# Scores of two heads from the two row halves of the array, in an attention-and-MoE kernel on one core

## The chip, the cores and the metric

The kernel runs on one core of one Trainium2 chip. The core has a TensorE (PE in the profile) with its weight loads shown apart (PEld), a VectorE (DVE), a ScalarE (ACT), a GpSimd (POOL), and a SyncE (SP), whose queue issues all DMAs here. The metric is device time in microseconds, from the median of several runs.

## What is computed

Causal attention with a decay (8 batches, 8 heads, 576 tokens, head dimension 64) is followed by a feed-forward layer (512 to 2048 to 512) over all 4608 tokens, called the MoE in the code.

```python
def _attn_ref(q, k, v, f):
    scale = 1.0 / np.sqrt(D)
    scores = scale * np.matmul(q, k.transpose(0, 1, 3, 2))
    cum = np.cumsum(np.log(np.clip(f, 0.0001, 1.0)), axis=-1)
    decay = cum[:, :, :, None] - cum[:, :, None, :]
    scores = np.where(causal, -1000000000.0, scores + decay)
    ...
    attn = attn / (np.sum(attn, axis=-1, keepdims=True) + 1e-09)
    return np.matmul(attn, v)

def _moe_ref(x, w_in, w_out):
    h = x @ w_in
    g = np.where(pos, h, np.where(neg, 0.0, (h + beta) ** 2 / (4.0 * beta)))
    return g @ w_out
```

## The kernel before

**Jobs.** Two heads of a batch make a pair; a pair is a job, except in batch 0, whose pairs are cut into rows 0 to 255 and 256 to 575 (`CUTS`). That makes 36 jobs. The first 12 (`NQK`) compute their scores in float32, the other 24 in float16 from split operands: each number is a high float16 plus a low float16 that holds the rest.

**A job's stages.** `load` (L311) brings q and k of both heads into `x32`. `measure` (L385) finds the scale of q and k. `prepare` (L408) splits them into `qs` and turns `qs` with a transposing DMA into `qkT` (L430), so that the head dimension lies on partitions; the float32 jobs do this in `early_prepare` (L362) with TensorE transposes and copies by ScalarE (L381, L383). `scores(w, r)` (L466) makes row tile r of 128 query rows against all keys up to it: 128, 256, 384 or 512 columns for r = 0 to 3, each head into its own tile `s` in PSUM; the last row tile, r = 4, has 64 rows a head and 576 columns, and both heads share one tile `big`, head 0 on partitions 0 to 63 and head 1 on 64 to 127. GpSimd prepares the decay and the mask for the same tile (L496, L500). `weights` (L565) adds the two, takes the exponential and the sum, splits the result and turns it with another transposing DMA into `pT` (L609). `values` (L616) multiplies by v, the two heads into two column halves of the array.

**Score products before.** In float16, q of a head lies as high on rows 0 to 63 and low on rows 64 to 127; k lies doubled, the high part on both row halves and the low part on both (`kk`, doubled by the copy at L427). Two products of 128 rows then give all four terms (L492):

```python
for c in range(2):
    nc.tensor.matmul(
        sp[p0:p1, c0:c1], lhsT=w.q[:, h, ...],
        rhs=w.k[:, c, h, c0:c1], start=(c == 0), stop=(c == 1),
    )
```

In float32, k of the two heads lies stacked on the two row halves, and q of each head stands in its half of a buffer whose other half is zero (zeroed once, at L360), so one product of 128 rows gives one head (L486).

**MoE.** Work comes in units (`moe_front`, L650, with its products at L665, and `moe_back`, L686, products at L693). Units are handed out between the steps of the attention as tokens become ready; what is left runs after the last pair. The weights are split during the first jobs (`weight_split`, L188).

**What sets the order.** The code is written in the order of the loop at L765, with the next pair's preparation ahead of a pair's scores. A scheduler then orders each engine's instructions by priority and by when it expects buffers to be free. Every engine works in its order, and SP's queue issues DMAs in its order. The tile `s` has two buffers in PSUM, so the next row tile's scores wait until DVE has read the ones before (L579).

## Time and profile before

| | |
|---|---|
| median of 3 runs | 1213.34 us (1212.29 to 1214.77) |
| span of the profiled execution, first to last instruction | 1209.7 us |
| mean granted clock of TensorE | 0.941 |
| PE by slices of a fortieth of the span (tenths busy) | `4677678996598989999999999999799989999998` |
| score products, float16 (L492) | 576, from 291 to 1038 us |
| score products, float32 (L486) | 192 records, from 14 to 278 us |

The profiled execution has no time of its own beside its span; the runs' times lie a few microseconds above it. In the profile a line such as "L492 PE MATMUL s<-qkT 128\*128 128x512 f16" names the source line, the engine, what is written and read, the part of the array used (rows by columns), and the output's size. A row half is 64 rows of the array; a column half is 64 of its columns. A float32 product shows as two records.

### The profile page before, as it was taken

Reading aid. Unit: us, or ns where it says so; the run is one execution under the profiler, and the core shown is the slowest. Engines: PE = TensorE matmul, PEld = TensorE weight load, DVE = VectorE, ACT = ScalarE, POOL = GpSimd, SP = SyncE. Lnnn points to the kernel's source line nnn. Section 1 sums busy time; section 2 is a strip of 40 time slices with the busy share of each in tenths; the row PEclk is TensorE's granted clock in tenths of the full one; section 3 lists DMA queues with packets and bytes.
Section 4 is the critical chain, followed back from the end, with each engine's and each line's share of the span. In section 5 each row is a group of like instructions: output and inputs, shape, how many; then the busy total and the mean of one; then the engine's idle time right before and its main releaser. Section 6 shows DMA issues by size and latency. Waiting matters only on the chain. (4 is left out here: it accounts for less than half of the span.)

```text
span 1209.7 us, 24371 instructions
## 1 busy us (share of the span) xinstructions
PE 1074.8 (89%) x8577; PEld 707.0 (58%) x8577; DVE 865.9 (72%) x2447; ACT 766.1 (63%) x1570; POOL 445.6 (37%) x699
## 2 busy tenths in 40 slices
PE   4677678996598989999999999999799989999998
PEld 3454344663366656665666666666566666667665
DVE  6879979775887788877766867877878788532222
ACT  4675666774576677767666767776667587643443
POOL 5648634533444334423433234433543264100000
PEclk9878788998599998999899999999899989999999
DMA  8857544569787859685666656894969686400000
GB/s 239 255 170 178 133 121 96 122 131 193 158 159 130 172 119 179 130 181 124 133 131 138 137 106 142 160 190 106 179 117 189 127 161 113 96 18 2 18 18 18
DMA packets 439258, 160.04 MB, mean 132 GB/s; under 512 B 414944, under 2 KB 415968, under 8 KB 439136
## 3 DMA queue, kind: packets, MB, share of 16 engines
q1 hardware_dynamic: 439136, 158.49, 61.2%
q8 instruction: 67, 1.10, 0.4%
q14 instruction: 55, 0.45, 0.1%
HBM read 75.64 MB, written 9.58 MB: 70 GB/s over the span
## 5 line engine op out<-in xcount | busy, mean ns | idle before, releaser
L665 PE MATMUL ph<-x,place 128*128 128x256 f16 (+3 forms) x4608 | 454.2, 251 | 15.9 <-DVE u L676 8.7
L693 PE MATMUL po<-place,g 128*128 128x512 f16 x1728 | 423.6, 383 | 12.0 <-DVE g L679 5.9
L665 PEld LDWEIGHTS <-place 128*128 128x128 f16 x4608 | 371.7, 100 | 99.8 <-issue 25.1
L693 PEld LDWEIGHTS <-g 128*128 128x128 f16 x1728 | 162.9, 98 | 179.1 <-DVE g L679 10.5
L496 POOL TENSOR_SCALAR sdr<-ck,nsig,cqs 128x128 f32<-128x128 f32 (+1 forms) x192 | 161.0, 842 | 200.4 <-DVE pr L603 184.3
L583 ACT ACTIVATE sdr<-sdr,nm 128x384 f32<-128x384 f32 (+1 forms) x248 | 138.2, 558 | 105.7 <-DVE nm L579 99.0
L676 DVE SCALAR_TENSOR_TENSOR u<-ph,z,u 128x512 f32<-128x512 f32 x136 | 101.3, 745 | 106.2 <-ACT u L675 105.6
L674 ACT ACTIVATE u<-ph,z 128x512 f32<-128x512 f32 x136 | 104.5, 768 | 92.6 <-PE ph L665 92.5
L678 ACT ACTIVATE g<-u,z 128x512 f16<-128x512 f32 x136 | 97.6, 717 | 91.7 <-DVE u L676 91.5
L597 ACT ACTIVATE pr<-sdr,rc 128x384 f16<-128x384 f32 (+1 forms) x236 | 119.2, 555 | 44.3 <-issue 19.2
L496 POOL TENSOR_SCALAR sd<-ck,nsig,cqs 64x576 f32<-64x576 f32 x48 | 50.7, 1057 | 259.2 <-DMA ck<-cum_d 77.1
L603 DVE SCALAR_TENSOR_TENSOR pr<-sdr,rc,pr 128x384 f16<-128x384 f32 (+2 forms) x232 | 124.2, 568 | 14.7 <-ACT pr L597 14.0
L679 DVE SCALAR_TENSOR_TENSOR g<-u,z,g 128x512 f16<-128x512 f32 x136 | 105.9, 779 | 37.7 <-ACT g L678 37.3
L579 DVE CUSTOM_DVE_ANT_0 sdr<-s,sdr,nalpha 128x128 f32<-128x128 f32 (+1 forms) x192 | 102.4, 543 | 20.5 <-PE s L492 10.2
L492 PE MATMUL s<-qkT 128*128 128x128 f16 (+3 forms) x384 | 87.2, 320 | 24.0 <-DVE nm L579 13.6
L500 POOL TENSOR_SCALAR_AFFINE_SELECT sdr<-sdr 128x128 f32<-128x128 f32 x248 | 92.8, 386 | 9.6
L675 ACT ACTIVATE u<-u 128x512 f32<-128x512 f32 x144 | 89.9, 625 | 2.9
L492 PEld LDWEIGHTS <-qkT 128*128 128x128 f16 (+1 forms) x576 | 47.3, 104 | 66.5 <-issue 43.7
L623 PE MATMUL big<-pT,vs 128*64 128x320 f16 (+3 forms) x1098 | 74.7, 286 | 5.5 <-DVE nm L579 4.6
L392 DVE TENSOR_REDUCE m2q<-qk 128x1 f32<-128x640 f32 x48 | 39.1, 817 | 50.4 <-DMA qk<-in_q_dram 26.1
L623 PEld LDWEIGHTS <-vs 128*64 128x64 f16 x1098 | 53.4, 113 | 32.6 <-issue 13.4
L496 POOL TENSOR_SCALAR sdr<-ck,cq 128x384 f32<-128x384 f32 (+3 forms) x56 | 40.0, 714 | 67.5 <-DVE pr L603 23.3
(168 smaller groups left out, 1180.6 us busy)
## 6 DMA issues: line engine op xcount, KB each, us to landing
ck<-cum_d SPq DMA_DIRECT2D x64, 288.0 KB, 3.8
out_dram<-ot SPq DMA_DIRECT2D x36, 256.0 KB, 2.4
qk<-in_k_dram SPq DMA_DIRECT2D x64, 128.0 KB, 2.9
ck<-in_v_dram SPq DMA_DIRECT2D x28, 288.0 KB, 3.1
v<-in_v_dram SPq DMA_DIRECT2D x62, 128.0 KB, 2.6
qk<-in_q_dram SPq DMA_DIRECT2D x56, 128.0 KB, 2.7
place<-in_moe_w_in_dram SPq DMA_DIRECT2D x12, 512.0 KB, 4.9
place<-in_moe_w_out_dram SPq DMA_DIRECT2D x10, 512.0 KB, 6.3
```

What stands on the lines that cost most here:

```text
L492: nc.tensor.matmul(sp[p0:p1, c0:c1], lhsT=w.q[:, h, q0 - w.s0:q0 - w.s0 + p1 - p0], rhs=w.k[:, c, h, c0:c1], start=(c == 0), stop=(c == 1),)
L496: nc.gpsimd.tensor_scalar(out=sd[p0:p1, 0:wid], in0=w.ck[h][p0:p1, 0:wid], scalar1=w.nsig if w.p < NQK else w.nsig[p0:p1], scalar2=w.cqs[p ...
L579: nc.vector.tensor_tensor_reduce(out=a, in0=sp[:, 0:wid], in1=a, scale=w.nalpha, scalar=BIG, op0=ALU.add, op1=ALU.min, accum_out=nm[:, i:i ...
L583: nc.scalar.activation(a, a, AF.Exp, bias=nm[:, i:i + 1], scale=-1.0, accum_out=sm[:, i:i + 1])
L597: nc.scalar.activation(pr[:, :, 0, i, :], a, AF.Copy, scale=rc[:, i:i + 1])
L603: nc.vector.scalar_tensor_tensor(out=pr[:, :, 1, i, :], in0=a, scalar=rc[:, i:i + 1], in1=pr[:, :, 0, i, :], op0=ALU.mult, op1=ALU.subtract,)
L623: nc.tensor.matmul(av[64 * h:64 * h + 64, at + s0:at + s1], lhsT=w.vs[:, vl, h, t, :], rhs=w.pT[:, t, pl, h, s0:s1], start=(t == 0 and pi ...
L665: nc.tensor.matmul(ph[:, fi, a0:a1], lhsT=wi[fb][:, wl, t, fi * P:(fi + 1) * P], rhs=xs[b][:, t, xl, s0:s0 + a1 - a0], start=(fi == 0 and ...
L674: nc.scalar.activation(u, h, AF.Relu, scale=z.u[:, i:i + 1], bias=z.h[:, i:i + 1])
L676: nc.vector.scalar_tensor_tensor(out=u, in0=h, scalar=z.t[:, i:i + 1], in1=u, op0=ALU.max, op1=ALU.min)
L679: nc.vector.scalar_tensor_tensor(out=g[:, 1], in0=u, scalar=z.r[:, i:i + 1], in1=g[:, 0], op0=ALU.mult, op1=ALU.subtract)
L693: nc.tensor.matmul(po[ch][i], lhsT=g[:, gl, fi * TC + i * P:fi * TC + (i + 1) * P], rhs=wo[fb][:, wl, fi, :], start=(first and fi == 0 and ...
```

## The change

In float16, `qs` now has four blocks of 640 columns: q high, q low, k high, k low, each with the two heads side by side, so that after the transposing DMA head 0 lies on rows 0 to 63 and head 1 on rows 64 to 127. A head's scores are three products of 64 rows (high by high, low by high, high by low; the term low by low is no longer computed), head 0 in the upper row half of the array and head 1 in the lower. In float32 q and k lie stacked alike and one product of 64 rows makes a head. The doubled k with its copy, the zeroed halves with their memsets, and the copies of half height go. The transposing DMA of a pair has 20 blocks of 128 by 128 instead of 30. In `scores` the products of both heads are written in turn, ahead of the GpSimd work of both. `load` puts the float16 jobs' q and k into the layout of the float32 ones (token tile, head, dimension).

```diff
@@ load
-            if ji < NQK:
-                dst = x.rearrange("p (t h d) -> p h t d", t=nt, h=2)
-            else:
-                dst = x.rearrange("p (h t d) -> p h t d", t=nt, h=2)
-                if ji < max(NQK, ncut) + 2 and w.r1 == NT5:
-                    nc.gpsimd.memset(dst[64:P, :, nt - 1, :], 0.0)
+            dst = x.rearrange("p (t h d) -> p h t d", t=nt, h=2)
+            if NQK <= ji < max(NQK, ncut) + 2 and w.r1 == NT5:
+                nc.gpsimd.memset(dst[64:P, :, nt - 1, :], 0.0)
...
-    early_qk = [two.tile([P, 3, 2, SP], F16, name="qkT") for i in range(2)]
+    early_qk = [two.tile([P, 4, SP], F16, name="qkT") for i in range(2)]
...
-    for t in early_qk:
-        for h in range(2):
-            nc.gpsimd.memset(t[64 - 64 * h:128 - 64 * h, h, :], 0.0)
@@ early_prepare
-        w.q, w.k = t_, t_[:, 2]
+        w.terms = ((t_[:, 0], t_[:, 1]),)
...
-            if j == 0:
-                for h in range(2):
-                    rows = slice(64 * h, 64 * h + 64)
-                    nc.scalar.activation(t_[rows, h, 0:n], pt[rows, 0:n], AF.Copy)
-            else:
-                nc.scalar.activation(t_[:, 2, 0:n], pt[:, 0:n], AF.Copy)
+            nc.scalar.activation(t_[:, j, 0:n], pt[:, 0:n], AF.Copy)
@@ prepare
...
-        dup = kk.rearrange("p c b e -> p (c b) e")
-        nc.vector.tensor_copy(dup[:, :, D:P], dup[:, :, 0:D])
...
+        qs = one.tile([P, 4, NT5 * P], F16, name="qs")
+        for j in range(2):
+            nc.scalar.activation(qs[:, 2 * j], w.x32[j], AF.Copy, scale=sc[:, j:j + 1])
+        for j in range(2):
+            nc.vector.scalar_tensor_tensor(
+                out=qs[:, 2 * j + 1], in0=w.x32[j], scalar=sc[:, j:j + 1], in1=qs[:, 2 * j],
+                op0=ALU.mult, op1=ALU.subtract,
+            )
+        qkT = two.tile([P, 4, SP], F16, name="qkT")
+        nc.sync.dma_start_transpose(
+            qkT.rearrange("p c (b e) -> p (c b) e", e=P), qs.rearrange("p c e -> p (c e)")
+        )
+        qh, ql, kh, kl = (qkT[:, c] for c in range(4))
+        w.terms = ((qh, kh), (ql, kh), (qh, kl))
@@ scores
-            for c0 in range(0, wid, 512):
-                c1 = min(wid, c0 + 512)
-                if w.p < NQK:
...
-                for c in range(2):
-                    nc.tensor.matmul(
-                        sp[p0:p1, c0:c1], lhsT=w.q[:, h, q0 - w.s0:q0 - w.s0 + p1 - p0],
-                        rhs=w.k[:, c, h, c0:c1], start=(c == 0), stop=(c == 1),
-                    )
+        for c0 in range(0, wid, 512):
+            c1 = min(wid, c0 + 512)
+            for i, (a, b) in enumerate(w.terms):
+                for h, (p0, p1) in enumerate(at):
+                    rows = slice(64 * h, 64 * h + 64)
                     nc.tensor.matmul(
+                        sds[h % len(sds)][1][p0:p1, c0:c1], lhsT=a[rows, q0 - w.s0:q0 - w.s0 + p1 - p0],
+                        rhs=b[rows, c0:c1], start=(i == 0), stop=(i == len(w.terms) - 1),
                     )
+        for h, (p0, p1) in enumerate(at):
+            sd = sds[h % len(sds)][0]
```

What the scheduler makes of it on PE, at row tile r = 2 (384 columns) of the ninth float16 pair. `qkT` holds the pair's q and k, the two tiles `s` are head 0's and head 1's, `g` and `po` belong to the MoE. Before:

```order
L492 LDWEIGHTS qkT_6491
L492 MATMUL s_6984<-qkT_6491 128x384
L492 LDWEIGHTS qkT_6491
L492 MATMUL s_6984<-qkT_6491 128x384
L693 LDWEIGHTS g_7242
L693 MATMUL po0_6677<-place13_103,g_7242 128x512
L492 LDWEIGHTS qkT_6491
L492 MATMUL s_6991<-qkT_6491 128x384
L492 LDWEIGHTS qkT_6491
L492 MATMUL s_6991<-qkT_6491 128x384
```

And in the change, on the same engine at the same place:

```order
L470 MATMUL s_7058<-qkT_6550 128x384
L470 LDWEIGHTS qkT_6550
L470 MATMUL s_7058<-qkT_6550 128x384
L470 LDWEIGHTS qkT_6550
L470 MATMUL s_7058<-qkT_6550 128x384
L673 LDWEIGHTS g_7324
L673 MATMUL po0_6744<-place13_103,g_7324 128x512
L470 LDWEIGHTS qkT_6550
L470 MATMUL s_7059<-qkT_6550 128x384
L470 LDWEIGHTS qkT_6550
L470 MATMUL s_7059<-qkT_6550 128x384
L470 LDWEIGHTS qkT_6550
```

Although the code writes the heads in turn, head 0's three products stand together, then a product of the MoE (L673 is L693 of before), then head 1's three.

Row tile r = 0 (128 columns) of the same pair, on PE in the change, where `ph` is the MoE's (L645 is L665 of before):

```order
L645 MATMUL ph_7295<-x_3196,place12_102 128x256
L470 LDWEIGHTS qkT_6550
L470 MATMUL s_7010<-qkT_6550 128x128
L470 LDWEIGHTS qkT_6550
L470 MATMUL s_7011<-qkT_6550 128x128
L470 LDWEIGHTS qkT_6550
L470 MATMUL s_7010<-qkT_6550 128x128
L470 LDWEIGHTS qkT_6550
L470 MATMUL s_7011<-qkT_6550 128x128
```

Here the heads alternate, as written, with nothing between them; before, two products of each head stood there one after the other.

On DVE, where the same pair is split into `qs`, before:

```order
L420 SCALAR_TENSOR_TENSOR qs_6485<-qk32_0_114,sc_6397,qs_6485 128x10x64
L404 RECIPROCAL nalpha_6405<-nsig_6403 128x1
L423 SCALAR_TENSOR_TENSOR qs_6485<-qk32_0_114,sc_6397,qs_6485 128x10x64
L427 COPY qs_6485<-qs_6485 128x20x64
L676 SCALAR_TENSOR_TENSOR u_6458<-ph_6409,z_5528,u_6458 128x512
```

And in the change:

```order
L405 SCALAR_TENSOR_TENSOR qs_6545<-qk32_0_114,sc_6457,qs_6545 128x640
L559 ISA sdr_2_119,nm_6617<-s_6568,sdr_2_119,nalpha_5948 128x256
L559 ISA nm_6617 128x1
L405 SCALAR_TENSOR_TENSOR qs_6545<-qk32_0_114,sc_6457,qs_6545 128x640
L571 TENSOR_SCALAR rc_6592<-sm2_6587 128x2
```

The two subtractions stay, each over 640 columns in one piece; the doubling copy is gone, and a reading of scores (L559, L579 of before) now stands between the two.

More of the change, by code (lines that the diff above doesn't have):

```diff
@@ L354 @@
     prs = [one.tile([P, PRN[r]], F16, name=f"pr{r}").bitcast(F32) for r in range(NT5)]
-    early_qk = [two.tile([P, 3, 2, SP], F16, name="qkT") for i in range(2)]
-    early_qk = [t.rearrange("p c h s -> p (c h s)").bitcast(F32)[:, 0:3 * S].rearrange("p (c s) -> p c s", c=3) for t in early_qk]
+    early_qk = [two.tile([P, 4, SP], F16, name="qkT") for i in range(2)]
+    early_qk = [t.rearrange("p c s -> p (c s)").bitcast(F32)[:, 0:2 * S].rearrange("p (c s) -> p c s", c=2) for t in early_qk]
     cq8 = const.tile([P, NT5, 2 * H], F32, name="cq8")
-    for t in early_qk:
-        for h in range(2):
-            nc.gpsimd.memset(t[64 - 64 * h:128 - 64 * h, h, :], 0.0)
     def early_prepare(w):
@@ L411, in prepare @@
         sc = w.sc
-        nq, nk = w.r1 - w.r0, w.r1
-        qs = one.tile([P, 3, 2, NT5, P], F16, name="qs").rearrange("p c h t e -> p (c h t e)")
-        nqe = 2 * nq * P
-        qq = qs[:, 0:nqe].rearrange("p (b e) -> p b e", e=P)
-        kk = qs[:, nqe:nqe + 4 * nk * P].rearrange("p (c b e) -> p c b e", c=2, e=P)
-        xq, xk = (x.rearrange("p (b d) -> p b d", d=D) for x in w.x32)
-        nc.scalar.activation(qq[:, :, 0:D], xq, AF.Copy, scale=sc[:, 0:1])
-        nc.scalar.activation(kk[:, 0, :, 0:D], xk, AF.Copy, scale=sc[:, 1:2])
-        nc.vector.scalar_tensor_tensor(
-            out=qq[:, :, D:P], in0=xq, scalar=sc[:, 0:1], in1=qq[:, :, 0:D], op0=ALU.mult, op1=ALU.subtract
-        )
-        nc.vector.scalar_tensor_tensor(
-            out=kk[:, 1, :, 0:D], in0=xk, scalar=sc[:, 1:2], in1=kk[:, 0, :, 0:D], op0=ALU.mult, op1=ALU.subtract
-        )
-        dup = kk.rearrange("p c b e -> p (c b) e")
-        nc.vector.tensor_copy(dup[:, :, D:P], dup[:, :, 0:D])
-        n = nqe + 4 * nk * P
-        qkT = two.tile([P, 3, 2, SP], F16, name="qkT").rearrange("p c h s -> p (c h s)")
-        nc.sync.dma_start_transpose(qkT[:, 0:n].rearrange("p (b e) -> p b e", e=P), qs[:, 0:n])
-        w.q = qkT[:, 0:nqe].rearrange("p (h s) -> p h s", h=2)
-        w.k = qkT[:, nqe:n].rearrange("p (c h s) -> p c h s", c=2, h=2)
+        qs = one.tile([P, 4, NT5 * P], F16, name="qs")
[9 more added lines that the diff above has]
+            qkT.rearrange("p c (b e) -> p (c b) e", e=P), qs.rearrange("p c e -> p (c e)")
+        )
+        qh, ql, kh, kl = (qkT[:, c] for c in range(4))
+        w.terms = ((qh, kh), (ql, kh), (qh, kl))
     def split_values(w):
@@ L469, in scores @@
         q0 = P * r
-        sds = []
+        sds, at = [], []
         for h in range(2):
-            p0, p1 = (0, P) if r < LAST else (64 * h, 64 * h + 64)
+            at.append((0, P) if r < LAST else (64 * h, 64 * h + 64))
             if r < LAST or h == 0:
```

4 lines of the change are left out of this document (removed).

## The prediction

> **What bounds the kernel now.** I read the page first, then busy time by stretch, then who PE waits for.
>
> ```profile
> span 1209.7 us, 24371 instructions
> PE 1074.8 (89%) x8577; PEld 707.0 (58%) x8577; DVE 865.9 (72%) x2447; ACT 766.1 (63%) x1570; POOL 445.6 (37%) x699
> ```
>
> ```profile
> 0.00:291.00 291.00, 218.80 (x1283) 135.61 (x1284) 236.48 (x712) 184.50 (x410) 154.68 (x228) 0.88 0.64 163
> 291.00:1040.00 749.00, 691.28 (x5948) 459.16 (x5945) 578.73 (x1664) 508.50 (x1055) 290.90 (x472) 0.95 0.73 145
> 1040.00:1209.70 169.70, 164.76 (x1353) 112.19 (x1351) 50.71 (x73) 73.10 (x106) 0.00 (x0) 1.00 0.09 23
> 290.00:400.00 110.00, 82.19 (x743) 55.19 (x742) 82.22 (x252) 66.02 (x145) 46.93 (x71) 0.83 0.82 158
> 600.00:700.00 100.00, 99.63 (x820) 66.00 (x819) 70.23 (x199) 64.14 (x124) 26.99 (x45) 1.00 0.65 132
> 700.00:800.00 100.00, 99.04 (x732) 63.17 (x731) 78.41 (x212) 73.32 (x152) 42.02 (x68) 1.00 0.71 142
> ```
>
> The columns after the length are busy time of PE, PEld, DVE, ACT and POOL, then PE's granted clock, DMA share and GB/s. There are three phases. To 291 us the twelve float32 jobs run beside the splitting of the weights, and DVE is busiest (236 of 291). From 291 to 1040 us the 24 float16 pairs run among the MoE products: PE is busy 691 of 749 us, so only 58 us are free, 28 of them before 400 us and 1.4 between 600 and 800. After 1040 us PE does MoE alone. Scores are computed only in the first two phases. In the second, what PE gains or loses is nearly all time; DVE, ACT and POOL have 170 us or more to spare there.
>
> ```profile
> PE s L492 <- DVE nm L579: 13.6, 15, 6.2
> PE s L492 <- DVE mk L131: 10.2, 5, 3.5
> ```
>
> Those are the longest waits of PE in the second phase (total us, times, longest): little of it is waiting for a free score buffer.
>
> **How PE's time is read.** Its busy times have modelled ends, so I use starts, from the timeline.
>
> ```profile
> 703.52 0.59 PE L492 MATMUL s<-qkT 128*128 128x512 f16 x2
> 703.95 1.25 PE L665 MATMUL ph<-x,place 128*128 128x256 f16 x10
> 705.04 0.59 PE L492 MATMUL s<-qkT 128*128 128x512 f16 x2
> 705.47 0.71 PE L665 MATMUL ph<-x,place 128*128 128x256 f16 x5
> 706.11 0.68 PE L492 MATMUL big<-qkT 128*64 128x512 f16 x5
> ```
>
> Two score products of 512 columns take 0.43 us to the next start: 0.215 each, 0.42 ns a column. Ten of 256 take 1.09, 0.109 each. Going from scores to MoE and back costs nothing, as both use the array whole (`128*128`). The last step differs: five products should take 0.545 us but the next starts 0.64 after, at a product in another form, `128*64`. So **a change of form costs 0.094 us**. The same holds for row halves:
>
> ```profile
> 223.50 0.27 PE L665 MATMUL ph<-x,place 128*128 128x256 f16 x1
> 223.61 0.80 PE L377 MATMUL big<-ident,qk 128*128 128x128 f32 x5
> 223.83 0.59 PE L377 MATMUL big<-ident,qk 128*128 128x128 f32 x3
> 224.34 0.28 PE L665 MATMUL ph<-x,place 128*128 128x256 f16 x1
> ```
>
> The fifth transpose reads 64 rows (the last 64 tokens). Two full ones take 0.22 us; the last three take 0.51 instead of 0.33, 0.18 more: one change into the 64-row form, one out of it.
>
> The Trainium skill, "TensorEngine Tiling (Array Packing)", section "Key Properties", says that a change of tiling mode drains TensorE while a change of tile does not. The trace agrees, at 0.094 us; without that cost the sum below would be 34 us lower, which is a rival.
>
> **Edit 1: products of r 0 to 3, float16.** What two halves of the array do together, only column halves show:
>
> ```profile
> 989.11 0.38 PE L693 MATMUL po<-place,g 128*128 128x512 f16 x1
> 989.42 2.25 PE L623 MATMUL big<-pT,vs 128*64 128x64 f16 x36
> 991.60 0.60 PE L693 MATMUL po<-place,g 128*128 128x512 f16 x2
> ```
>
> The 36 products of one pair's values have 2 x 4800 columns (three times 64 + 512 + 448 + 320 + 192 + 64 a head), 4.0 us in turn; they take 2.18. So halves run side by side, if no other form stands between them. Two row halves at once no row shows; the bounds are side by side (as here) and in turn, and I take side by side, the nearest row.
>
> Now the order decides. I went through PE's order of the change and asked, for each float16 row tile, whether both heads' products stand in one run of the 64-row form. They do in 21 of 96 (9 of 128 columns, 7 of 256, 2 of 384, 3 of 512), partly in one, and not in 74 (14, 17, 22, 21): there a whole-array product stands between three products of one head and three of the other. A tile costs 4 products in turn before; now 3 when together, 6 when apart. Apart: 25,344 columns, two products more; together: 5,248, one less; net 45,440 x 0.42 ns = +19.1. Where a tile's last head meets the next tile's first head in one run, these overlap too, -1.0 by the same count: **+18.1 us**. If row halves never overlap, the 21 tiles cost two more instead of one less, +6.6, and the 1.0 is lost.
>
> **Edit 2: the last tile (r = 4).**
>
> ```profile
> 460.91 0.69 PE L492 MATMUL big<-qkT 128*64 128x512 f16 x8
> ```
>
> Its eight products have 2304 columns, 0.97 us in turn, yet all are over in 0.69: the heads already ran side by side in column halves, though written one after the other. Three products a head instead of two make this 3 x 576 x 0.42 = 0.73 instead of 0.48. Before, 16 of 24 blocks are cut by other work and lose overlap; now 13. Run by run, counting the longer head of each run, the 24 blocks make 17.1 us before and 19.2 now: **+2.1**. In turn they would make 24 x 1.46 = 35.0, another +15.8.
>
> The Trainium skill, same page, section "Gotcha 1: PSUM Pressure", says that different row tiles cannot access one PSUM bank at once, and the two heads of r = 4 write one bank. No run here shows that case; by the rule it would come out in turn, the third rival.
>
> **Edit 3: float32 products.**
>
> ```profile
> 225.01 1.02 PE L486 MATMUL s<-qkT 128*128 128x512 f32 x2
> 225.87 0.60 PE L665 MATMUL ph<-x,place 128*128 128x256 f16 x4
> ```
>
> One product is two records: 0.86 us, 1.68 ns a column. Together now are 13 of 32 row tiles (4352 columns): -7.3; heads of neighbouring tiles in one run, -1.4: **-8.7**. Its eight blocks of r = 4 stay at 576 x 1.68 = 0.97 us, the heads side by side. In turn all that is lost.
>
> **Edit 4: changes of form.** Counted over PE's order, leaving out one-column transposes, they go from 309 to 670, as each score run of r 0 to 3 is now an island in MoE work: 74 more before the first float16 score (+7.0) and 288 more among the float16 pairs (**+27.1**), one less after.
>
> **Edit 5: what goes elsewhere.**
>
> ```profile
> L427 DVE COPY qs<-qs 128x1280 f16<-128x1280 f16 x24 | 11.9, 498 | 0.0
> ```
>
> ```profile
> L430 SPq DMA_TRANSPOSE qkT<-qs x24: 4430/4688/5285, 276.7 to 1005.0; - x24
> L381 ACT ACTIVATE qkT<-big x24: 361/432/646, 11.4 to 250.4; 64x256 f32<-64x256 f32 x8, 64x320 f32<-64x320 f32 x8, 64x576 f32<-64x576 f32 x8
> ```
>
> The copy goes: 11.9 us of DVE. The transposing DMA has 20 blocks instead of 30: by share, an estimate, 4.7 x 1/3 = 1.6 us less of SP's issue each, 37 us in all. Twelve fewer half-height copies save ACT some 5 us. All lie beside PE: where PE is the bound they are worth nothing. The cover would be gone if DVE set the pace; then the copy is worth 12 us at most, and SP's issue whatever of these waits is its doing:
>
> ```profile
> DVE m2q L392 <- DMA qk<-in_k_dram: 23.7, 14, 3.4
> DVE m2q L392 <- DMA qk<-in_q_dram: 23.4, 15, 3.5
> ```
>
> At the start something is on the path:
>
> ```profile
> 4.73 2.45 POOL L360 MEMSET qkT<- 64x576 f32 x4
> 4.93 1.59 DVE L246 TENSOR_REDUCE m<-x 128x1 f32<-128x576 f32 x2 [0.34 <-DMA x<-in_v_dram]
> 7.74 1.35 DVE L151 TENSOR_TENSOR_SCAN x<-x 64x576 f32<-64x576 f32 x1 [1.22 <-POOL x L149]
> ```
>
> The scan waits for POOL's next memset, which stands behind the four that go; then DVE's own reduce, over at 6.52, is late next: **-1.2**.
>
> Waits added: the heads' products are now written interleaved, but the order keeps a head's three behind one wait, so PE's waits for score buffers stay; zero, or 13.6 us either way. Weight loads rise by 288; where stream is 0.054 us (128 columns) a load could show, 0 to 6.5 us; I take 0, as the 128-column pairs of before hide theirs.
>
> **The sum.** First phase: -1.2 - 8.7 + 7.0 = -2.9. Second: 18.1 + 2.1 + 27.1 = +47.3. Some of that falls into PE's 58 free microseconds. Spread evenly it is 6.3 per 100 us: I let half vanish in 290 to 400 (3.5), a third in 400 to 600 and 800 to 1040 (9), none between, 12.5 in all. 1209.7 - 2.9 + 47.3 - 12.5 = 1241.6 against the span; the median of the runs, 1213.34, lies 3.6 above that span, which I add as what lies around it. Predicted: **1245 us**.
>
> **The rivals.**
> - *Row halves, or two heads in one bank, run in turn.* One bank: +15.8 and, for the eight float32 blocks, +7.8: 1269. All: another 6.6 + 1.0 + 8.7: 1285. Against both: column halves write one bank together. Chances 0.10 for the bank (1262 to 1276), 0.07 for all (to 1290). The first is what the rule of section "Gotcha 1" of the Trainium skill would bring.
> - *Changes cost less when PE has work queued.* Without the 34 us, and a quarter of the remaining 20 absorbed: 1213.3 - 9.9 + 15 = 1218. Against it: they cost 0.094 in dense stretches too. Chance 0.09.
> - *PE's free time swallows all.* 47 fit into 58: 1213 less 2.9, about 1211 to 1215. Against it: 600 to 800 us has no room. Chance 0.06.
> - *Faster: the pace is DVE's.* If a pair's period follows the chain load, measure, split, transpose, PE's 47 us hide and the 11.9 us copy comes off: 1213.3 - 2.9 - 11.9 = 1198. It decides if PE's free time in the second phase exceeds the 47 added. For it: DVE's 47 us of waits on loads; against it: DVE is busy 70 of 100 us where PE is full. Chance 0.08.
>
> **How the numbers follow.** Forecast 0.60, 1228 to 1262 (all absorbed but a third, to none and a few unknown loads). The range for 8 in 10 leaves out the faster and the equal case and the top of the first rival: 1222 to 1280. A difference under 0.2%, the spread of the three runs, cannot be told from none: slower 0.86, same 0.06, faster 0.08.
>
> **What would show it.** In the changed profile: starts of a lone head's three products 0.215 apart at 512 columns, and 0.094 more at both ends of the run; two heads' products of one run starting together; r = 4 blocks of 12 products about 0.25 longer; PE free time in the second phase below 58; the phase about 35 longer, the MoE tail unchanged. I am wrong if lone runs show no 0.094, or if the phase keeps its length with PE nearly full.

## The result and the profile after

| | before | change |
|---|---|---|
| median, runs side by side | 1214.05 us (1210.72 to 1215.66, 6 runs) | 1222.88 us (1221.13 to 1228.38, 6 runs) |
| change over before | | 1.0077, 95% interval 1.0052 to 1.0102 |
| span of the profiled execution | 1209.7 us | 1221.4 us |
| mean granted clock of TensorE | 0.941 | 0.954 |

The change is slower, by 8.8 us instead of the 31.7 that were predicted. The page of the changed kernel:

```profile
span 1221.4 us, 24896 instructions
PE 1118.6 (92%) x8865; PEld 683.2 (56%) x8865; DVE 854.6 (70%) x2423; ACT 762.5 (62%) x1558; POOL 443.9 (36%) x695
```

The same stretches as in the prediction (length, busy time of PE, PEld, DVE, ACT, POOL, then PE's granted clock, DMA share, GB/s):

```profile
0.00:291.00 291.00, 223.65 (x1273) 126.88 (x1274) 233.31 (x712) 176.98 (x396) 156.87 (x226) 0.87 0.66 164
291.00:1040.00 749.00, 717.77 (x6166) 438.19 (x6166) 562.95 (x1621) 502.79 (x1035) 284.75 (x467) 0.98 0.67 134
1040.00:1221.40 181.40, 177.13 (x1428) 118.08 (x1426) 58.32 (x91) 82.74 (x129) 2.25 (x5) 1.00 0.10 25
```

In the second phase PE was free for 58 us before and is free for 31 now, and its clock stands at 0.98 instead of 0.95. PE's own steps show in its timeline, first two lone heads of 512 columns (row tile 3), then both heads of a row tile of 128 columns in one run, then an r = 4 block:

```profile
706.42 0.27 PE L645 MATMUL ph<-x,place 128*128 128x256 f16 x1
706.63 0.82 PE L470 MATMUL s<-qkT 64*128 64x512 f16 x3
707.38 1.16 PE L645 MATMUL ph<-x,place 128*128 128x256 f16 x9
708.47 0.82 PE L470 MATMUL s<-qkT 64*128 64x512 f16 x3
709.22 1.38 PE L645 MATMUL ph<-x,place 128*128 128x256 f16 x11
...
548.02 0.34 PE L470 MATMUL s<-qkT 64*128 64x128 f16 x6
548.30 1.92 PE L645 MATMUL ph<-x,place 128*128 128x256 f16 x16
...
866.52 0.93 PE L470 MATMUL big<-qkT 64*64 64x512 f16 x12
867.38 1.85 PE L645 MATMUL ph<-x,place 128*128 128x64 f16 x30
```

Between 706.42 and 706.63 stands one product of 256 columns: 0.21 us instead of 0.109, a change of form. The lone head's three products take 0.75, three times 0.215 and a change of form back. The six products of 548.02 take 0.28 us, near the 0.16 + 0.09 of three products of 128 columns and a change of form and not the 0.42 of six in turn, so the two heads run side by side. The twelve of r = 4 take 0.86, near the 0.73 + 0.09 of heads side by side and far from the 1.46 of heads in turn.

So PE's float16 work grew as foretold. To see what took it up, I split PE's time by its starts: a product's columns at full clock ("work"), 0.094 us at each change of form, what a granted clock below full adds, and the rest, in which PE waits. From the first to the last float16 score product, in us:

| | length | work | changes of form | waits | clock |
|---|---|---|---|---|---|
| before, 292.9 to 1037.6 | 744.7 | 629.2 | 19.1 | 79.2 | 19.2 |
| change, 287.6 to 1052.1 | 764.5 | 657.7 | 45.9 | 51.6 | 10.7 |

The four parts are counted from starts and overshoot the lengths by 1 to 2 us. 55 us of work and changes came, and 36 us of waits and lowered clock went, against the 12.5 that the prediction let vanish. PE's waits for DVE (the order of columns is total us, times, longest):

```profile
PE s L470 <- DVE nm L559: 13.3, 8, 6.1
...
PE s L470 <- DVE mk L131: 1.5, 1, 1.5
```

The second row was 10.2 us before. `mk` is DVE's copy of a small product that serves the measuring of a later pair; that product is written into a tile `s` like the scores, so the next scores can't have the tile until the copy is done. DVE's own waits for DMAs, in the same stretch, 291 to 1010 us:

```profile
DVE m2q L381 <- DMA qk<-in_q_dram: 31.9, 15, 3.8
...
DVE m L246 <- DMA ck<-in_v_dram: 19.3, 15, 3.3
...
DVE m2q L381 <- DMA qk<-in_k_dram: 7.0, 8, 1.5
```

For q and k it waits 38.9 us, 47.1 before. And the transposing DMA's issue on SP fell from 4.7 us (median) to 3.2, as estimated:

```profile
L410 SPq DMA_TRANSPOSE qkT<-qs x24: 3000/3170/4479, 273.5 to 1010.2; - x24
```

The question for the experiments: is the missing 23 us a better absorption of the products, or is the lighter preparation, which the prediction priced at nothing, worth something?

### The profile page after: what moved, and what is told of

It is laid out like the page before. It is cut to its first block, busy times and chain, and to the rows that moved or that the text cites. A ratio compares the mean times of both kernels' runs of the same rounds, so it can differ in the third digit from the quotient of the medians.

```text
span 1221.4 us, 24896 instructions
## 1 busy us (share of the span) xinstructions
PE 1118.6 (92%) x8865; PEld 683.2 (56%) x8865; DVE 854.6 (70%) x2423; ACT 762.5 (62%) x1558; POOL 443.9 (36%) x695
## 3 DMA queue, kind: packets, MB, share of 16 engines
q1 hardware_dynamic: 408416, 150.63, 57.7%
## 4 chain that ended last, share of the span: by engine, by line
PE 38%; DVE 5%; DMA 3%; issue 2%; SPq 2%; ACT 2%; POOL 0%; DVEq 0%; ACTq 0%
PE ph L645 16%; PE po L673 16%; PE s L470 3%; PE big L603 2%; DMA ck<-in_v_dram 1%; DVE pr L583 1%; DVE sdr L559 1%; SPq L332 1%; DMA qk<-in_k_dram 1%; PE big L470 1%; DMA qk<-in_q_dram 1%; DVE u L656 1%; DVE g L659 1%; SPq L429 0%; ACT pr L577 0%
## 5 line engine op out<-in xcount | busy, mean ns | idle before, releaser
L645 PE MATMUL ph<-x,place 128*128 128x256 f16 (+3 forms) x4608 | 449.9, 250 | 12.6 <-DVE u L656 7.9
L673 PE MATMUL po<-place,g 128*128 128x512 f16 x1728 | 423.7, 384 | 9.4 <-DVE g L659 5.8
L645 PEld LDWEIGHTS <-place 128*128 128x128 f16 x4608 | 356.0, 99 | 115.2 <-issue 44.8
L673 PEld LDWEIGHTS <-g 128*128 128x128 f16 x1728 | 161.3, 99 | 184.8 <-issue 21.1
L476 POOL TENSOR_SCALAR sdr<-ck,nsig,cqs 128x128 f32<-128x128 f32 (+1 forms) x192 | 155.9, 815 | 229.8 <-DVE pr L583 218.1
L470 PE MATMUL s<-qkT 64*128 64x384 f16 (+6 forms) x704 | 158.9, 359 | 23.3 <-DVE nm L559 21.6
L476 POOL TENSOR_SCALAR sd<-ck,nsig,cqs 64x576 f32<-64x576 f32 x48 | 54.2, 1130 | 242.6 <-ACT qs L403 91.0
L559 DVE CUSTOM_DVE_ANT_0 sdr<-s,sdr,nalpha 128x128 f32<-128x128 f32 (+1 forms) x192 | 103.2, 545 | 23.1 <-PE s L470 17.0
L470 PEld LDWEIGHTS <-qkT 64*128 64x128 f16 (+1 forms) x864 | 47.9, 99 | 88.0 <-issue 66.5
L603 PEld LDWEIGHTS <-vs 128*64 128x64 f16 x1098 | 49.9, 112 | 28.8 <-issue 10.1
```

Of the source, the lines that this page charges most:

```text
L470: nc.tensor.matmul(sds[h % len(sds)][1][p0:p1, c0:c1], lhsT=a[rows, q0 - w.s0:q0 - w.s0 + p1 - p0], rhs=b[rows, c0:c1], start=(i == 0), st ...
L476: nc.gpsimd.tensor_scalar(out=sd[p0:p1, 0:wid], in0=w.ck[h][p0:p1, 0:wid], scalar1=w.nsig if w.p < NQK else w.nsig[p0:p1], scalar2=w.cqs[p ...
L559: nc.vector.tensor_tensor_reduce(out=a, in0=sp[:, 0:wid], in1=a, scale=w.nalpha, scalar=BIG, op0=ALU.add, op1=ALU.min, accum_out=nm[:, i:i ...
L603: nc.tensor.matmul(av[64 * h:64 * h + 64, at + s0:at + s1], lhsT=w.vs[:, vl, h, t, :], rhs=w.pT[:, t, pl, h, s0:s1], start=(t == 0 and pi ...
L645: nc.tensor.matmul(ph[:, fi, a0:a1], lhsT=wi[fb][:, wl, t, fi * P:(fi + 1) * P], rhs=xs[b][:, t, xl, s0:s0 + a1 - a0], start=(fi == 0 and ...
L673: nc.tensor.matmul(po[ch][i], lhsT=g[:, gl, fi * TC + i * P:fi * TC + (i + 1) * P], rhs=wo[fb][:, wl, fi, :], start=(first and fi == 0 and ...
```

## The experiments

Times are medians; ratios are to runs of the kernel before that ran beside it on the same chip. Differences between two variants are of medians, sometimes from different chips; by the ratios they come out up to 2.5 us smaller.

### One half of the change at a time

**e1**, the change's preparation with products over the whole array; **e2**, the change's 64-row products on the preparation of before.

```diff
@@ e1, against the change
-                    rows = slice(64 * h, 64 * h + 64)
...
-                        sds[h % len(sds)][1][p0:p1, c0:c1], lhsT=a[rows, q0 - w.s0:q0 - w.s0 + p1 - p0],
-                        rhs=b[rows, c0:c1], start=(i == 0), stop=(i == len(w.terms) - 1),
+                        sds[h % len(sds)][1][p0:p1, c0:c1], lhsT=a[:, q0 - w.s0:q0 - w.s0 + p1 - p0],
+                        rhs=b[:, c0:c1], start=(i == 0), stop=(i == len(terms) - 1),
@@ e2, against before
-                for c in range(2):
+            cs = (None,) if w.p < NQK else (0, 1, 1)
+            for i, c in enumerate(cs):
+                for h, (p0, p1) in enumerate(at):
+                    rows = slice(64 * h, 64 * h + 64)
...
+                        sds[h % len(sds)][1][p0:p1, c0:c1], lhsT=w.q[rows, h, q0 - w.s0:q0 - w.s0 + p1 - p0],
+                        rhs=w.k[rows, c0:c1] if c is None else w.k[rows, c, h, c0:c1],
```

> The preparation of the change (stacked q and k, no doubling copy, 20 blocks in the transposing DMA, no zeroed halves, whole copies) with the products of before: whole-array form, one per head in float32, two per head in float16. The scores are not those of the kernel, since a whole-array product adds both heads, and one float16 term is left out. PE's work, counted by columns and changes of form, is 985.6 us against 984.1 before. Theory A (PE's added work vanished into its own waits and into fewer throttled stretches, the preparation is worth little): 1206 to 1213 against 1214 before, mostly from the first phase. Theory R (the preparation's relief of DVE, SP and ACT paid for some 24 us of PE's added work): 1187 to 1197, with PE's waits in the second phase down from 79 us to about 55.

> The products of the change (64-row form, three per head in float16, one in float32, heads in turn) on the preparation of before, with its copy, 30 blocks and memsets. The float16 scores leave out some terms and count one twice. PE's work is counted 1028.6 us, as in the change (1029.5) and 44.5 above before. Theory A: 1220 to 1228, like the change (1223) or up to 5 above for the first phase. Theory R: 1240 to 1250, as then nothing pays for PE's added work but the 12 us that I had allowed.

| | products of before | 64-row products |
|---|---|---|
| preparation of before | 1214.4 | e2: 1238.8 (1.0199, 1.0179 to 1.0219) |
| preparation of the change | e1: 1191.9 (0.9809, 0.9768 to 0.9851) | the change: 1222.9 (1.0077, 1.0052 to 1.0102) |

The products alone cost 24.4 us. The preparation alone gains 22.5, and 15.9 on top of the products. So e1 lies where theory R had it; e2 lies 1.2 us below R's range and 10.8 above A's. The pages show that e1 does the work of before on PE and that e2 does that of the change:

```profile
span 1183.3 us, 24302 instructions
...
PE 1063.0 (90%) x8577; PEld 697.1 (59%) x8577; DVE 853.8 (72%) x2423; ACT 758.3 (64%) x1558; POOL 437.0 (37%) x695
```

```profile
span 1235.7 us, 24949 instructions
...
PE 1127.7 (91%) x8865; PEld 690.4 (56%) x8865; DVE 861.7 (70%) x2447; ACT 771.3 (62%) x1570; POOL 441.8 (36%) x699
```

By the split of PE's time, e1's second phase has the work of before (627.9, changes 18.8) and 66.9 us of waits instead of 79.2, not the 55 of theory R, in an execution that was 6.8 us faster than e1's median; e2's has 652.8, 46.2 and 58.9.

**e3** and **e8** try two parts that came along in these halves: the order of the code in `scores` (the heads' products in turn, in e2, and GpSimd's work behind them, in both), and the layout in which q and k are loaded (with the memsets of the loaded tiles, in e1).

```diff
@@ e3, against before
-            for c0 in range(0, wid, 512):
...
-                for c in range(2):
+        for c0 in range(0, wid, 512):
+            c1 = min(wid, c0 + 512)
+            cs = (None,) if w.p < NQK else (0, 1)
+            for i, c in enumerate(cs):
+                for h, (p0, p1) in enumerate(at):
@@ e8, against before
-                dst = x.rearrange("p (h t d) -> p h t d", t=nt, h=2)
-                if ji < max(NQK, ncut) + 2 and w.r1 == NT5:
-                    nc.gpsimd.memset(dst[64:P, :, nt - 1, :], 0.0)
+            dst = x.rearrange("p (t h d) -> p h t d", t=nt, h=2)
+            if NQK <= ji < max(NQK, ncut) + 2 and w.r1 == NT5:
+                nc.gpsimd.memset(dst[64:P, :, nt - 1, :], 0.0)
```

> The kernel of before with nothing changed but the order of the code in scores: products of both heads written in turn, GpSimd's work of both behind them. PE's work is counted 981.5 us against 984.1. Theories A and R: 1209 to 1217 (before 1214). Theory S (the other order that the scheduler makes is what shortened PE's waits): below 1205, with PE's waits in the second phase near the 52 us of the change instead of 79.

> The kernel of before with the change's loading alone: the float16 jobs' q and k in the layout of the float32 ones, so that the four memsets of L332 have nothing to wait for and move from 219 to 256 us to the start of POOL's order. Copy, 30 blocks, zeroed halves and 128-row products as before; the blocks of qs follow the token tiles. If the moved memsets or the layout were the preparation's gain: 1192 to 1202 (before 1214). If not: 1210 to 1217.

e3: 1216.5, ratio 1.0025 (1.0004 to 1.0045). e8: 1216.9, 1.0011 (0.9992 to 1.0029). Neither is the cause. Each edit also makes the scheduler find a new order for all engines; in these two that moved the time by some 2 us.

### The float32 jobs alone

**e4** has the change in the twelve float32 jobs alone. **e11** is e4 with the doubling copy on GpSimd. **e10** is e1 with the first phase as before (zeroed halves, copies of half height).

```diff
-        nc.vector.tensor_copy(dup[:, :, D:P], dup[:, :, 0:D])
+        nc.gpsimd.tensor_copy(dup[:, :, D:P], dup[:, :, 0:D])
```

> The change in the twelve float32 jobs alone (stacked q, no memsets, whole copies, 64-row products of both heads in turn), the float16 pairs as before. In the change the first float16 product started 5 us earlier than before. If the first phase is a gain of its own: 1207 to 1211 (before 1214). If its 5 us are only MoE work that moved out of it: 1212 to 1216.

> As e1 in the float16 pairs (loading, split without a copy, 20 blocks; the same scores left out), but the first phase as before: zeroed halves, copies of half height, 128-row float32 products (the second zeroed half in a buffer of its own). If the preparation's gain came in the first phase (zeroed halves and half copies): 1205 to 1214. If it came with the float16 pairs: 1190 to 1200.

> e4 (the change in the float32 jobs alone, 128-row float16 products of before) with the doubling copy moved from DVE to GpSimd. PE's work as in e4. If DVE's half microsecond is what holds the second phase in the presence of 30 blocks: 1190 to 1200 (e4 1205). If the length of the chain split, copy, transposing DMA, first score holds it: 1205 or above, as GpSimd's copy is slower than DVE's. A version that would beat before and change.

e4: 1205.4 (1196.2 to 1209.5, 8 runs), 0.9917 (0.9886 to 0.9949). The change's float32 part is a gain by itself, somewhat more than was expected of it. e10: 1196.9, 0.9852 (0.9815 to 0.9888), so of e1's 22.5 us the float32 jobs' part has about 5 and the float16 preparation 17.5. e11: 1208.9 (1201.3 to 1216.3, 10 runs), 0.9948 (0.9914 to 0.9981): DVE is rid of the copy and nothing is gained over e4; GpSimd's copy takes 1.25 us where DVE's took 0.50. Both spread widely, so a few us between them mean nothing.

### PE's work made less

**e7** gives both heads one tile of two banks in PSUM, one buffer of it, so that a row tile's heads must stand together. The small products of the measuring use the same buffer.

```diff
-        pt = ps.tile([P, 512], F32, name="s")
+        pt = ps1.tile([P, 2, 512], F32, name="s")[:, 0]
...
-                    sp = ps.tile([P, 512], F32, name="s")
+                    if h == 0:
+                        both = ps1.tile([P, 2, 512], F32, name="s")
+                    sp = both[:, h]
```

> The change, with one score tile of two banks for both heads in place of two tiles of one bank, so that both heads' products of r 0 to 3 become ready at once. In the order their six products then stand in one run nearly everywhere: changes of form fall from 670 to 520, and PE's work is counted 975.9 us (change 1029.5, before 984.1). If the parting of the heads is where the change lost its gain on PE: 1180 to 1200, some half to three quarters of the 53 us below 1223. If the waits for a tile that both heads must leave free cost more than that: 1215 or above, with PE's waits for DVE in the second phase up by 20 us or more.

1263.1, ratio 1.0411 (1.0377 to 1.0445): 40 us slower than the change, with less to do on PE. Work and changes of form in the second phase fell from 703.6 to 657.6 us, waits rose from 51.6 to 103.3 and what the clock takes from 10.7 to 23.4. Here are e7's second phase and its longest waits of PE:

```profile
291.00:1040.00 749.00, 661.20 (x5780) 419.61 (x5778) 547.07 (x1557) 475.62 (x983) 256.27 (x440) 0.93 0.65 130
```

```profile
PE s L472 <- DVE nm L561: 20.2, 9, 6.7
PE s L120 <- DVE nm L561: 17.7, 5, 5.2
PE s L130 <- DVE dg L127: 10.7, 6, 4.8
```

PE waits for DVE to have read both heads (`nm`), and the last two rows are the small products (L120, L130) that share the buffer. A share of PE's work is not the time's measure: a kernel with 46 us less of it is the slowest of all.

### Copy and transposed blocks

The float16 preparation has two large parts: the copy that goes from DVE and ten transposed blocks that go from SP's queue. Each was put back, alone and together, on e1 and on the change; the copy copies a tile onto itself, the ten blocks turn a zeroed tile.

```diff
@@ copy (e5 on e1, e17 on the change; e13 twice, on e1)
+        nc.vector.tensor_copy(qs[:, 0:2], qs[:, 0:2])
@@ blocks (e6 on e1, e16 on the change; both in e9 and e12)
+    qs6 = const.tile([P, 6, NT5 * P], F16, name="qs")
...
-        qs = one.tile([P, 4, NT5 * P], F16, name="qs")
+        qs = qs6
+        if w.p == NQK:
+            nc.gpsimd.memset(qs[:, 4:6], 0.0)
...
-        qkT = two.tile([P, 4, SP], F16, name="qkT")
+        qkT = two.tile([P, 6, SP], F16, name="qkT")
```

> As e1 (preparation of the change, whole-array products of before; the same scores are left out), with a copy of 1280 columns put back ahead of the transposing DMA: qs onto itself, 0.5 us of DVE each, 24 times. If the copy was what the preparation saved in the second phase: e1's 1191.9 plus 10 to 16. If it was the ten blocks of the DMA: within 4 of 1191.9. PE's work is counted 982.6 us (e1 985.6).

> As e1, with the transposing DMA back at 30 blocks: ten of zeros, never read, behind the twenty. If the blocks were what the preparation saved: 1191.9 plus 10 to 16, and the issue of the DMA back at 4.7 us on SP. If it was the copy: within 4 of 1191.9.

> As e1, with both put back: the copy of 1280 columns on DVE and the ten more blocks of the transposing DMA. If either alone found room where both together would not: 1200 or above (e1 1191.9, before 1214). If neither matters: 1183 to 1196, as e1, e5 and e6.

> The change with the copy of 1280 columns and the ten blocks put back (qs onto itself, zeros never read). On e1 the two together cost 13.3. If they cost the same where PE has the change's products: 1232 to 1240, near e2 (1239), and the preparation accounts for the difference between e2 and the change. If PE's fuller order hides them: 1221 to 1226.

> The change's preparation with the products of before over the whole array, as in e1 (so the scores are not the right ones: the two heads are added up and one of the float16 terms is missing), with the 1280-column VectorE copy put back twice (about 1.0 us of VectorE a pair instead of 0.5; nothing of the second copy is used). One such copy alone cost nothing (1190.4 beside 1191.9), copy and ten transposed blocks together 13. Theory A (VectorE has a small reserve a pair, and whatever exceeds it shows, from wherever it comes): the second copy uses up the reserve as the ten blocks did, about 1203. Theory B (the copy's cost needs the longer transposing DMA behind it, since only the chain split - copy - DMA has a threshold): again nothing, 1188 to 1194.

> The change with ten transposed blocks put back (30 a pair), without the copy. The change is 1222.9, with copy and blocks 1237.9. Theory A (each has a cost of its own here): 1228 to 1232. Theory B (only together, as on the preparation alone, where the blocks alone were -6 and the copy alone -1.5): 1220 to 1225. Theory C (the blocks alone carry it, SyncE's queue): 1236 to 1240.

> The change with the VectorE copy of 1280 columns put back, 20 blocks. Theory A (each has a cost of its own): 1228 to 1232. Theory B (only together): 1220 to 1225. Theory C (the copy alone carries it, VectorE's time): 1234 to 1240.

| put back | neither | copy | blocks | both |
|---|---|---|---|---|
| on e1 | 1191.9 | 1190.4 (0.9822, 0.9786 to 0.9859); twice 1191.9 (0.9806, 0.9783 to 0.983) | 1185.8 (0.9779, 0.9742 to 0.9816) | 1205.2 (0.9922, 0.9895 to 0.995) |
| on the change | 1222.9 | 1218.7 (1.003, 1.001 to 1.005) | 1237.3 (1.0175, 1.0153 to 1.0197) | 1237.9 (1.0178, 1.0127 to 1.0229) |

On the change the answer is plain: the **ten blocks** alone cost 14.4 us, and 19.2 where the copy is there in both kernels (e17, e12). The copy, 0.5 us of DVE a pair, costs nothing; with it alone the change is even 4 us faster, which none of the three theories had. With the blocks back the change is e2 again (1238.8), so they are nearly all of the preparation's worth there. On e1 either part alone costs nothing and both together 13; two copies cost nothing too, so it isn't an amount of DVE's time that decides there. A copy that makes the change 4 us faster also shows that a new order can move the time by more than the 2 us of e3 and e8; the 6 us by which the blocks alone lie below e1 are within the spread of e1's runs. On e1, DVE's waits go the same way as the time. With blocks alone, and with both:

```profile
DVE m2q L383 <- DMA qk<-in_q_dram: 30.6, 15, 4.3
...
DVE m2q L383 <- DMA qk<-in_k_dram: 9.1, 9, 2.3
```

```profile
DVE m2q L383 <- DMA qk<-in_q_dram: 41.6, 17, 5.3
DVE m2q L383 <- DMA qk<-in_k_dram: 19.3, 13, 3.4
```

39.7 us and 60.9; e1 itself has 40.6. Why the order that came out with the blocks alone waits less there was not settled.

### The way from the blocks to the end

In the change with blocks (e16) `qkT` is issued 11 us or more before the pair's first score product and lands in 6 to 8, and no row of PE's waits names its DMA, so the blocks are not late themselves. SP's queue in e16, at one pair:

```profile
622.48 1.09 SPq L334 DMA_DIRECT2D qk<-in_q_dram  x2
623.61 1.16 SPq L338 DMA_DIRECT2D qk<-in_q_dram  x1
624.87 4.55 SPq L414 DMA_TRANSPOSE qkT<-qs  x1
629.46 1.16 SPq L334 DMA_DIRECT2D qk<-in_k_dram  x2
630.67 0.62 SPq L338 DMA_DIRECT2D qk<-in_k_dram  x1
```

and DVE at the same place (what is in brackets is the idle time before the instruction and what ended it):

```profile
625.07 0.16 DVE L578 RECIPROCAL rc<-rc 128x2 f32<-128x2 f32 x1
626.89 0.82 DVE L383 TENSOR_REDUCE m2q<-qk 128x1 f32<-128x640 f32 x1 [1.67 <-DMA qk<-in_q_dram]
627.63 0.47 DVE L563 CUSTOM_DVE_ANT_0 sdr<-s,sdr,nalpha 128x256 f32<-128x256 f32 x1
...
633.36 0.82 DVE L383 TENSOR_REDUCE m2q<-qk 128x1 f32<-128x640 f32 x1 [0.46 <-DMA qk<-in_k_dram]
```

The loads of a later pair stand around the transposing DMA, k behind its 4.55 us. DVE's order has the measuring (`m2q`) right behind these loads although its result is wanted only when that pair is prepared, and all that stands behind it on DVE is late, here a reading of scores (`sdr` from `s`). At this place the longer wait is for q, ahead of the transposing DMA. Over the phase the waits for k rise from 7.0 us in the change to 18.3 in e16, while those for q fall from 31.9 to 28.3.

What PE waits for in e16 is less the scores' reading than `mk`, the measuring's own copy:

```profile
PE s L474 <- DVE mk L131: 9.8, 4, 4.4
PE s L474 <- DVE nm L563: 7.9, 6, 5.4
```

In the change these were 1.5 and 13.3. With the copy in both, e17 and e12, `mk` goes from 1.3 to 10.5. The longest of these waits in e16:

```profile
322.66 0.82 DVE L383 TENSOR_REDUCE m2q<-qk 128x1 f32<-128x640 f32 x1 [3.60 <-DMA qk<-in_k_dram]
...
325.93 0.15 DVE L131 COPY mk<-s 128x2 f32<-128x2 f32 x1
326.13 0.48 PE L474 MATMUL s<-qkT 64*128 64x128 f16 x3 [4.40 <-DVE mk L131]
```

DVE stands 3.60 us for k of a later pair, `mk` stands behind that in DVE's order, and PE waits 4.40 us for the tile. Two kernels try to take such waits away. **e18** gives the change three buffers for q and k, each load a pair earlier. **e19** takes e16 and ties the measuring to a later point of the pair.

```diff
@@ e18, against the change
-    qk32 = [const.tile([P, 2, 2, NT5, D], F32, name=f"qk32_{i}") for i in range(2)]
+    qk32 = [const.tile([P, 2, 2, NT5, D], F32, name=f"qk32_{i}") for i in range(3)]
...
-            if p + 2 < njobs:
-                pairs.append(load(p + 2))
+            if p + 3 < njobs:
+                pairs.append(load(p + 3))
@@ e19, against e16
         m2 = tiny.tile([P, 2], F32, name="m2q")
+        nc.vector.tensor_copy(m2, after)
...
         rc = tiny.tile([P, 2], F32, name="rc", bufs=8)
+        if r < w.r1 - 1:
+            w.rc = rc
...
-                    measure(pairs[p + 2])
+                    measure(pairs[p + 2], w.rc)
```

> The change with three instead of two buffers for q and k as they are loaded, each pair's load written one pair earlier (the space that the smaller qkT and qs leave). In the trace of the change with thirty blocks SyncE's queue has the loads of pair p+2 split around the transposing DMA of pair p+1 (q ahead of it, k behind its 4.55 us), and VectorE, whose order has the measuring of pair p+2 soon after, stands waiting for them. Theory A (the blocks' cost comes to VectorE through these loads): VectorE's waits for q and k in the second phase, 38.9 us in the change, fall below 10, and the time falls by a third of that or more, to 1200 to 1212. Theory B (the waits only move: VectorE is then late somewhere else, or PE sets the end): the waits go and the time stays, 1217 to 1228.

> The change with thirty blocks (1237.3), and the measuring of the pair after next tied to the last full row tile of the pair at hand: its result tile is first written with that row tile's reciprocal sums (one VectorE copy of two columns a pair, overwritten at once), so VectorE's order can't have the two reductions right behind the loads, of which three are issued behind the transposing DMA. In the kernel with thirty blocks VectorE waits 46.6 us for loads of q and k in the second phase, 38.9 us with twenty. Theory A (the ten blocks reach VectorE through these loads): the waits fall below 15, and the time falls by 10 or more, to 1227 or less. Theory B (VectorE's waits for loads are not what the blocks cost; waits move elsewhere): the waits fall and the time stays, 1233 to 1241, or rises because the scale of the next pair comes later.

e18: 1231.9, ratio 1.0169 (1.0141 to 1.0198), slower than the change, and no test of the theory, because the waits stayed:

```profile
DVE m2q L381 <- DMA qk<-in_q_dram: 26.8, 15, 3.5
...
DVE m2q L381 <- DMA qk<-in_k_dram: 12.6, 11, 2.6
```

39.4 us, as in the change: the loads are again issued around the transposing DMA, and the measuring again follows at once. Its second phase is 8.5 us shorter (756.0), but the first float16 product comes 13.4 us later (301.0).

e19: **1214.5**, ratio 0.9999 (0.998 to 1.0019), 22.8 us less than e16 with the same thirty blocks and the same products. DVE's waits in e16, then in e19:

```profile
DVE m2q L383 <- DMA qk<-in_q_dram: 28.3, 13, 4.0
DVE m L246 <- DMA ck<-in_v_dram: 24.4, 16, 5.0
...
DVE m2q L383 <- DMA qk<-in_k_dram: 18.3, 13, 3.6
```

```profile
DVE sdr L564 <- PE s L475: 29.2, 39, 2.6
DVE m L246 <- DMA ck<-in_v_dram: 23.7, 16, 3.0
```

The 46.6 us for q and k are gone in e19: none of DVE's rows has `m2q`, and DVE now waits for PE first of all. PE's longest row is `nm`, as long as in e16, and it has no row of `mk`:

```profile
PE s L475 <- DVE nm L564: 8.3, 9, 4.7
```

The second phase, 291 to 1040 us, of e16 and of e19:

```profile
291.00:1040.00 749.00, 709.87 (x6022) 435.15 (x6020) 555.10 (x1601) 495.12 (x1016) 274.88 (x458) 0.96 0.72 142
```

```profile
291.00:1040.00 749.00, 723.12 (x6212) 443.36 (x6213) 577.93 (x1659) 510.24 (x1050) 283.87 (x470) 0.97 0.73 145
```

In the same 749 us DVE does 23 us more and PE 13 us more. PE's waits by the split fall from 57.7 to 42.6. So the order in which DVE meets these loads does cost time, though PE is busy 95% of the phase, and the row of PE's waits that goes is `mk`.

That the ten blocks' cost goes this way is likely, but not shown. The rows of `mk` speak for it. Against it as the whole account stand three things. Where the copy is in both kernels, the blocks cost 19.2 us while DVE's waits for q and k in total hardly change (40.5 us in e17, 41.9 in e12). Of the 14.3 us by which e16's span exceeds the change's, 5.6 lie ahead of the first float16 score product (293.2 against 287.6), where e19 gains nothing; its whole gain lies behind that product, and some 3.4 us of the gain are MoE products that now stand ahead of it. And the later measuring also removes the waits that the change with twenty blocks still has, and gives all engines a new order.

### A version without the copy

**e15** is e4 with no doubling copy: ScalarE writes the high part of k twice in one instruction, the low part stands once, its other half zeroed once. The product low by low is left out, as in the change.

```diff
-        nc.scalar.activation(kk[:, 0, :, 0:D], xk, AF.Copy, scale=sc[:, 1:2])
+        nc.scalar.activation(
+            kk[:, 0].rearrange("p b (x d) -> p b x d", x=2), xk.unsqueeze(2).broadcast_to([P, 2 * nk, 2, D]),
+            AF.Copy, scale=sc[:, 1:2],
+        )
...
-        nc.vector.tensor_copy(dup[:, :, D:P], dup[:, :, 0:D])
```

> e4 (the change in the twelve float32 jobs alone, 1205.4) with the doubling copy of the float16 jobs gone from VectorE: ScalarE writes high k in both halves in one write of 1280 columns a partition instead of 640, and low k only once, its second half zeroed once for all pairs (the product low by low is left out, as in the change). 30 blocks and 128-row products stay. Theory A (the copy on VectorE costs, with the thirty blocks there, about what copy and blocks cost together, 13 to 15): 1190 to 1194. Theory B (the copy is worth little by itself, as e11 with it on GpSimd showed, 1208.9): 1203 to 1209. ScalarE's longer write adds about 0.5 us a pair there, which would show as 1210 or more if ScalarE, which then holds VectorE's own input back, is the bound at that place.

1199.8 us (1196.3 to 1203.1), ratio 0.9878 (0.9849 to 0.9908): between the two theories' ranges, and faster than before and than the change. It keeps the float32 part and the whole-array float16 products. e15 with the later measuring of e19, and the change with it, were not run.

## Why the prediction was right and wrong

**Direction and range** were right; the size was not, 8.8 instead of 31.7 us. The 2 by 2 table says how it splits: the products alone give 24.4 instead of 31.7, and the preparation takes 15.9 off that the prediction put at zero. That 1222.9 lies in the range, 0.9 above its lower end, is luck: nothing in the range stood for a gain of the preparation.

**Edits 1, 2 and 4, the float16 products and the changes of form: right.** Second phase: work +28.5, of which some 5.4 are MoE products that moved in from the other phases, so 23 against 18.1 + 2.1; changes of form +26.8 against 27.1. First phase: changes +6.9 against +7.0, the start 1.3 us earlier (first product at 7.8 instead of 9.1) against 1.2. The rivals about PE's work fall: row halves and the two heads in one bank do run side by side, lone runs pay 0.094 at both ends, and with the products alone 24.4 us stay, so PE's free time doesn't swallow all.

**Edit 3, the float32 products: agreement by luck.** The first phase has 8.3 us less work, against 8.7 foretold, but 3.7 of that are MoE products that stand later now, so the float32 products gained about half. And in the 64-row form they have a cost that Edit 3 lacks:

```profile
224.43 1.12 PE L470 MATMUL s<-qkT 64*128 64x512 f32 x2
225.48 0.61 PE L645 MATMUL ph<-x,place 128*128 128x256 f16 x4
```

This product takes 1.05 us to the next start, 0.86 before; with 0.094 for the change of form, 0.10 is left, which shows in the other widths too as a longer step between the product's two records. For 13 tiles together and 19 apart that is 51 times 0.10, some 5 us, an estimate. The phase ends 5.3 us earlier against 2.9, but MoE products left it.

**The rules on drains and banks.** The Trainium skill, "TensorEngine Tiling (Array Packing)", section "Key Properties", says that changing the tiling mode drains TensorE; the changes of form measured here agree with it, at 0.094 us. The same page of the Trainium skill, section "Gotcha 1: PSUM Pressure", says that different row tiles cannot access one PSUM bank at once; this was not borne out here: the heads of r = 4 write one bank on other partitions, and their twelve products take 0.86 us, not the 1.46 of heads in turn.

**The failed step** is Edit 5: "All lie beside PE: where PE is the bound they are worth nothing." The rows that spoke against it stand in the prediction itself: DVE's 47 us of waits for loads, with SP's issue named as what would count if DVE set the pace, and PE's 10.2 us for `mk`. The step took "PE is busy 691 of 749 us" for a proof that PE is the bound. What the runs showed in its place: the lighter preparation is worth 15.9 us on top of the products (e2 against the change), and nearly all of that is the ten blocks of the transposing DMA (14.4, e16); the copy, priced there at 12 us at most, was worth nothing (e17, e5, e13). In a phase where PE is 95% busy, DVE still stands still for loads, the measuring's copy `mk` behind them is late, and PE waits for it; taking away the waits for q and k gave 22.8 us (e19).

**The sum's absorbed share** was mis-sized too. The products' 47.3 us were let vanish by 12.5, from PE's free time as a share of each stretch. With the preparation of before (e2), PE's waits shrank by 20.3 and what the clock took by 4.3 in the second phase, 24.6 together. A likely reading, which no run tried by itself, is that PE's waits for another engine shrink as PE's added work gives that engine time.

**The rival "faster: the pace is DVE's"** was near at the wrong place: DVE's waits on loads matter, its 11.9 us of copy don't, and the change doesn't become faster because 24 us of the products stay visible. Such a coupling beside a filled PE was not among the cases, which were either PE or DVE.

**Open:** why, on whole-array products, copy and blocks cost 13 us only together (e5, e6, e9), and how much of the blocks' cost goes through the loads of q and k and `mk`, rather than other entries of SP's queue or the order that the scheduler finds.

## What to carry to other kernels

A busy share of 92% on one engine doesn't make work elsewhere free: look at which instruction stands first in the waiting engine's order, and whether it is one that nobody needs yet. Half-array products save PE's time only where both halves stand together in the order; a lone half costs more columns and two changes of form, and forcing them together through a shared buffer cost more than it saved (e7). Where a change has a heavy and a light half, run each half alone before believing that one of them is nothing.

## What was not expected of the hardware

The granted clock changed with the kernel, and not simply with the sum of PE's waits. In the second phase it stood at 0.93 in e7 (103 us of waits, 23 lost to the clock), 0.95 before (79 and 19) and 0.98 in the change (52 and 11): in these three, a fifth to a quarter of the waits once more. But e19, with fewer waits than the change (43), had 0.97, and e1 had 0.97 with 67 us of waits where e16 had 0.96 with 58. What sets it no run tried. The Trainium skill, "TensorE: Matmul & The Clock Gate", section "Part 1: The HAM clock gate", says that idle time of TensorE brings the clock down; the first three traces agree in direction, the other three show that the total of waits doesn't decide. The sum of the prediction kept the clock as it was and so left out the 8.5 us by which its part fell (19.2 to 10.7).
